# GpSimd in place of ScalarE and SyncE as the asker for half of the gate and value weights

## The chip, the cores and the metric

The kernel runs on one core of a Trainium2 chip. The core's engines are TensorE (PE in the profile; PEld is its weight load), VectorE (DVE), ScalarE (ACT), GpSimd (POOL) and SyncE (SP). Each has its own queue of instructions and works through it in order; semaphores hold an instruction until what it needs is there. SP only asks for transfers here; ScalarE can ask for them too, and so can GpSimd. A transfer that one of them has asked for is carried out by 16 DMA engines, beside all other work. The metric is device time in microseconds (us); the time given for a kernel is the median of its runs.

## What is computed

An mLSTM cell over 4 batches, 8 heads, 768 time steps and a head size of 40, and a gated feed-forward block on its output:

```python
for t in range(S):                     # S = 768, for each batch and head
    m_new = np.maximum(f_gate[:, :, t] + m, i_gate[:, :, t])
    f_stab, i_stab = np.exp(f_gate[:, :, t] + m - m_new), np.exp(i_gate[:, :, t] - m_new)
    C = f_stab[..., None, None] * C + i_stab[..., None, None] * (vt outer kt)
    n = f_stab[..., None] * n + i_stab[..., None] * kt
    y[:, :, t] = sigmoid(o_gate[:, :, t]) * (C @ qt) / np.maximum(np.abs(n @ qt), 1.0)
x = y as (3072, 320)                   # tokens x (heads * head size)
g = x @ w_gate                         # (320, 1536)
out = (g * sigmoid(g) * (x @ w_val)) @ w_out
```

The inputs of the cell are float32. The three weight matrices are float64 in memory, and the kernel makes float32 of them itself.

## The kernel before

The 768 steps are cut into six groups (`NG`) of 128. In each group the cell runs in its parallel form (scores, a weight matrix, a carried state), and the group's 4 x 128 = 512 tokens then go through the feed-forward block. The order of all instructions is written out by hand; nothing is planned by a scheduler, so an engine's queue holds its instructions in the order of the Python calls that touch it.

**The opening, group 0.** Lines 619 to 666 interleave the first group's cell with the arrival of the first weights. Its weight matrix `W0` lies in the tile `h_sb` (blocks 0 to 7), `W0[:, u * H + h]` for batch u and head h; halves P = 0 and 1 are batches 0, 1 and 2, 3. For each half:

- `first_scores` (L565): PE makes scores, and DVE multiplies them into `W0` in place (L575, four instructions).
- `first_values` (L551): GpSimd copies the last column of `W0` (L552) and scales the values by it (L553). It reads that column before L575 of the same half overwrites it.
- `first_own` (L579), once per batch: PE multiplies `W0` with the values (L582). `first_x` (L584) divides on DVE, and `first_gate` (L593) multiplies by the output gate on DVE (L596) and has GpSimd copy 64 columns to the end of each row of `x_sb` (L597).
- `first_seam` (L610): PE transposes `x_sb` (L616), ten transposes of a half in three parts, and ScalarE, ScalarE and DVE copy the parts to `xT`. The last two transposes read the columns that L597 wrote.
- `first_state` (L599): PE, with GpSimd's `vw_sb`, makes the first carried state (L604).

`burn` (L518) is a matmul without use that keeps PE busy.

**The first feed-forward.** `hidden(0, m)` (L698), for the twelve blocks m of 128 hidden features: ten pairs of matmuls (L706), gate on partitions 0 to 63 and value on 64 to 127, then SiLU on ScalarE (L711) and a product on DVE (L712). The dictionaries `slots` and `ahead` say what is put between the blocks.

**Weights.** `PIECES` cuts the gate and value weights into seven pieces, of 1, 1, 2, 2, 2, 2 and 2 blocks, and the output weights into three. `piece_load(p)` (L161) asks for a piece. For a gate/value piece that is three transfers, in this order: the gate half to partitions 0 to 63 (320 rows of 128 or 256 float64), and the value half to partitions 64 to 127 in two parts, four chunks (64 x 4 rows) and one chunk (64 rows). The transfers come from line L187. The raw words go to a buffer named `raw` (two of them in turn, pieces 0, 1, 5 and 6), or to parts of `h_sb` (pieces 2 and 3) and `wo_sb` (piece 4) that are not in use yet. Piece 2's place is under the part of `W0` that batches 1 and 2 and half of batch 0 use, so its requests wait for `first_own(2)`. Pieces 5 and 6 wait until the blocks that lay in their buffer are scaled; all wait for an earlier transfer that had the same completion semaphore. SP and ScalarE draw these in turn from one set of eight, GpSimd from another set of eight.

A block j then becomes float32 in three steps: `scale(j)` (two ScalarE instructions, L212 and L214), `join(j)` (two DVE instructions, L221 and L222) and `rounded(j)` (L229; on GpSimd, and on DVE for blocks 0, 1, 2, 9, 10 and 11).

Pieces 0 to 5 are asked for in the opening (lines 636, 642, 645, 657, 665 and 666), piece 6 in `slots[1]`, after block 1. In the queue of SP the gate halves stand behind the loads of k, q, v and the output gate of group 0, and ahead of the loads of k for group 1, the write of `M_dram`, the loads of q, and (L484) the reading of `M_dram` into `w_sb`.

From group 1 on, the products of the feed-forward use seven multiplications in place of eight (`gated`, L847, and `project_seven`, L755); the change touches nothing there.

Of the kernel before, what the change touches and what calls it, by code (L numbers as in the profile page):

```python
# [24 lines left out]
def kernel(  # L25
# [18 lines left out]
    nc = tc.nc  # L44
# [116 lines left out]
    def piece_load(p, home=None):  # L161
        kind, m, n = PIECES[p]
        if kind == "gv":
            a, d = NKC, n * 128
            gate_w, val_w = (w[:, m * 128:(m + n) * 128].rearrange("(c p) f -> p c f", p=HP) for w in (moe_w_gate, moe_w_val))
            src = [(slice(0, HP), slice(0, NKC), gate_w), (slice(HP, 128), slice(0, NKC - 1), val_w[:, 1:]),
                   (slice(HP, 128), slice(NKC - 1, NKC), val_w[:, 0:1])]
            queues = (nc.sync,) + 2 * (nc.scalar if p < 5 else nc.sync,)
        else:
            a, d = n, DM  # L170
            src = [(slice(0, 128), slice(0, n), moe_w_out[m * 128:(m + n) * 128].rearrange("(a p) d -> p a d", p=128))]
            queues = (nc.sync,)
        if src[0][2].dtype == F32:
            for r, cs, w in src:
                if kind == "o":
                    nc.sync.dma_start(out=wo_sb[r, m:m + n, :], in_=w)
                else:
                    for x in range(n):
                        nc.sync.dma_start(out=wgv_sb[r, m + x, cs], in_=w[:, :, ts(x, 128)])
            return  # L180
        if home is None:
            raw = conv.tile([128, 4 * NKC * 128], U32, name="raw")
        else:
            raw = home.rearrange("p a t -> p (a t)").bitcast(U32)
        raw = raw[:, 0:2 * a * d]
        for (r, cs, w), queue in zip(src, queues):
            queue.dma_start(out=raw[r].rearrange("p (a d) -> p a d", a=a)[:, cs], in_=w.bitcast(U32))  # L187
        words = raw.rearrange("p (a d two) -> p a d two", two=2, a=a)
        raws[p] = (words[:, :, :, 0], words[:, :, :, 1])
        split(p)  # L190
# [4 lines left out]
    def split(p):  # L195
        if p in raws:
            lo, hi = raws.pop(p)
            kind, m, n = PIECES[p]
            if kind == "gv":
                for c in range(n):  # L200
                    r = slice(c * 128, (c + 1) * 128)
                    blocks[m + c] = (lo[:, :, r], hi[:, :, r], wgv_sb[:, m + c])
            else:
                for c in range(0, n, 2):
                    blocks[NFC + (m + c) // 2] = (lo[:, c:c + 2], hi[:, c:c + 2], wo_sb[:, m + c:m + c + 2, :])
# [428 lines left out]
    first_turn(1, q_sb, qT, (A, V))  # L634
    load(o_sb, o_gate, 0, 1)
    piece_load(0)
    first_own(1)
    first_values(1)
    first_scores(1)
    first_x(1)  # L640
    sig(0)
    piece_load(1)
    burn(3)
    first_own(2)
    piece_load(2, h_sb[:, 1:1 + NKC])
    sig(1)
    burn(2)
# [460 lines left out]
```

## Time and profile before

| | us |
|---|---|
| median of three runs | 512.6 |
| the runs | 513.2, 512.21, 512.6 |
| the profiled execution: device time | 513.3 |
| the profiled execution: span, first to last instruction | 511.5 |
| PE busy with L854 for gv_x from xT, 720 matmuls | 89.1 |
| PE busy with L706, 240 matmuls | 53.7 |
| value halves asked for by ScalarE: issue of one, median, into raw, h_sb, wo_sb | 0.65, 0.62, 0.55 |
| the same, from issue to landing, the larger part, into raw, h_sb, wo_sb | 4.0, 9.1, 11.6 |
| value halves asked for by SP: from issue to landing, larger and smaller part | 11.8, 10.4 |
| gate halves, from issue to landing, into raw (320 KB), h_sb, wo_sb, raw (640 KB) | 7.0, 11.7, 15.7, 8.9 |

How to read the profile: times are from the start of the span. A line of the timeline gives the start, the time from there to the end of the merged instructions, the engine, the line of the kernel, the operation, output and inputs, and how many instructions it merges; in brackets stands how long the engine was idle before, and what ended that. SPq and ACTq are the queues of SP and ScalarE, on which a request for a transfer is not counted as busy. A row of the table of windows gives a stretch, its length, then for PE, PEld, DVE, ACT and POOL the busy time and (the number of instructions), then the granted clock of PE, the share of the DMA engines, and GB/s. Ends of matmuls are modelled.

### The profile page before, as it was taken

The page shows a single profiled execution, that of the slowest core. Times are in us where ns is not written, and L with a number is a line of the kernel's source. Part 1 is how long each engine was busy: PE and PEld are TensorE (multiplying, and loading weights), DVE is VectorE, ACT ScalarE, POOL GpSimd, SP SyncE. Part 2 cuts the span into 40 slices and gives each one's busy share as a digit, 9 for nine tenths or more (in the row PEclk, how much of TensorE's full clock was granted, in tenths as well). Part 3 has the DMA queues.
Part 4 walks back from the last instruction along what each step waited for, and adds up shares of the span by engine and source line. Part 5 has one row for each costly group of instructions (what it writes and reads, how often), then busy time and mean ns, then how long its engine had stood idle before and what let it go on. Part 6 is the DMA issues. An engine that isn't in the chain of part 4 may idle for free.

```text
span 511.5 us, 14788 instructions
## 1 busy us (share of the span) xinstructions
PE 505.1 (99%) x6307; PEld 428.8 (84%) x6309; DVE 332.3 (65%) x539; ACT 204.8 (40%) x394; POOL 255.0 (50%) x274
## 2 busy tenths in 40 slices
PE   8999999999999999999999999999999999999997
PEld 4964445667888899988899888899988899988896
DVE  5779767887897777687466678467658554233421
ACT  3477655448512339312339321338421340223210
POOL 1303427475879663367652457652447650166710
PEclk9999999999999999999999999999999999999999
DMA  9999999698502992501993411993101200000001
GB/s 123 174 232 238 168 194 244 148 177 119 88 1 45 143 130 39 92 3 26 156 134 42 75 21 27 156 131 43 42 3 19 37 3 27 27 1 0 1 14 38
DMA packets 205497, 43.27 MB, mean 85 GB/s; under 512 B 193432, under 2 KB 200600, under 8 KB 205432
## 3 DMA queue, kind: packets, MB, share of 16 engines
q1 hardware_dynamic: 203444, 39.49, 49.4%
q10 hardware_dynamic: 1988, 2.85, 2.4%
q8 instruction: 49, 0.80, 0.7%
q14 instruction: 16, 0.13, 0.1%
HBM read 35.68 MB, written 4.01 MB: 78 GB/s over the span
## 4 chain that ended last, share of the span: by engine, by line
PE 91%; DMA 2%; DVE 2%; issue 1%; POOL 1%; ACT 1%; SPq 0%; DVEq 0%; ACTq 0%; POOLq 0%
PE gv_x L854 26%; PE o_ps L777 23%; PE gv_y L854 21%; PE gv_ps L706 5%; PE o_ps L723 5%; DMA w_sb<-M_dram 2%; PE inter L402 2%; PE intra L411 2%; PE sp L353 2%; PE first_y L582 1%; PE add L379 1%; POOL w_sb L493 1%; PE burn L521 1%; PE tp_kq L561 1%; PE sp L571 1%
## 5 line engine op out<-in xcount | busy, mean ns | idle before, releaser
L854 PE MATMUL gv_x<-xT,wgv_sb 64*128 64x256 f32 x720 | 89.1, 377 | 0.0
L854 PEld LDWEIGHTS gv_x<-xT,wgv_sb 64*128 64x128 f32 x720 | 69.6, 187 | 7.9 <-issue 0.2
L777 PE MATMUL o_ps<-wo_sb,h_sb 128*128 128x160 f32 x480 | 67.4, 300 | 0.0
L777 PEld LDWEIGHTS o_ps<-wo_sb,h_sb 128*128 128x128 f32 x480 | 65.6, 190 | 1.7 <-issue 1.7
L902 ACT ACTIVATE h_sb<-gv_x 128x256 f32<-128x256 f32 x30 | 11.5, 383 | 117.8 <-PE gv_x L854 117.8
L706 PE MATMUL gv_ps<-xT,wgv_sb 64*128 64x512 f32 x240 | 53.7, 596 | 0.3 <-DVE wgv_sb L229 0.3
L706 PEld LDWEIGHTS gv_ps<-xT,wgv_sb 64*128 64x128 f32 x240 | 23.6, 187 | 24.4 <-issue 23.2
L854 PE MATMUL gv_y<-q_sb,wgv_sb 64*128 64x256 f32 x360 | 44.0, 377 | 0.0
L854 PE MATMUL gv_y<-xT,wgv_sb 64*128 64x256 f32 x360 | 43.9, 376 | 0.0
L854 PEld LDWEIGHTS gv_y<-q_sb,wgv_sb 64*128 64x128 f32 x360 | 34.9, 187 | 4.2 <-DVE tmp L894 0.4
L854 PEld LDWEIGHTS gv_y<-xT,wgv_sb 64*128 64x128 f32 x360 | 35.0, 187 | 3.9
L364 POOL TENSOR_TENSOR vw_sb<-v_sb,w_sb 128x656 f32<-128x656 f32 x10 | 14.6, 1467 | 41.2 <-ACT w_sb L509 40.0
L777 PE MATMUL o_ps<-wT,S 128*128 128x160 f32 x240 | 33.4, 299 | 0.0
L777 PEld LDWEIGHTS o_ps<-wT,S 128*128 128x128 f32 x240 | 32.9, 190 | 0.0
L509 ACT ACTIVATE w_sb<-w_sb,g_T 128x64 f32<-128x64 f32 x128 | 31.0, 334 | 0.0
L854 PE MATMUL gv_x<-q_sb,sw 64*128 64x256 f32 x240 | 31.0, 376 | 0.0
L875 POOL TENSOR_TENSOR h_sb<-x_sb 128x512 f32<-128x512 f32 x12 | 15.8, 1314 | 24.6 <-ACT x_sb L874 24.6
L895 POOL TENSOR_TENSOR tmp<-tmp 128x512 f32<-128x512 f32 x15 | 20.0, 1332 | 14.5 <-DVE tmp L894 14.5
L875 POOL TENSOR_TENSOR h_sb<-tmp 128x512 f32<-128x512 f32 x13 | 16.5, 1269 | 21.5 <-ACT tmp L874 21.5
L744 POOL TENSOR_TENSOR S<-h_sb 128x256 f32<-128x256 f32 x30 | 22.6, 752 | 9.2 <-DVE h_sb L875 7.3
L854 PE MATMUL gv_y<-q_sb,sw 64*128 64x256 f32 x200 | 27.0, 388 | 0.0
L723 PE MATMUL o_ps<-wo_sb,h_sb 128*128 128x320 f32 x96 | 26.9, 437 | 0.0
(221 smaller groups left out, 984.6 us busy)
## 6 DMA issues: line engine op xcount, KB each, us to landing
w_sb<-M_dram SPq DMA_DIRECT2D x10, 512.0 KB, 7.1
k_sb<-in_k_dram SPq DMA_DIRECT2D x12, 320.0 KB, 7.4
v_sb<-in_v_dram SPq DMA_DIRECT2D x12, 320.0 KB, 5.5
o_sb<-in_o_gate_dram SPq DMA_DIRECT2D x12, 320.0 KB, 6.8
raw<-in_moe_w_out_dram SPq DMA_DIRECT2D x3, 1280.0 KB, 7.5
x_sq<-k_sb SPq DMA_DIRECT2D x64, 40.0 KB, 2.0
q_sb<-in_q_dram SPq DMA_DIRECT2D x32, 64.0 KB, 3.8
out_dram<-tmp SPq DMA_DIRECT2D x24, 80.0 KB, 1.7
```

The costliest lines, as they stand in the source:

```text
L353: nc.tensor.matmul(sp[two][half(i), a, :], lhsT=kT[feats(two), P * UA + a, half(i)], rhs=qT[feats(two), P * UA + a, half(i)], start=True, ...
L364: eng.tensor_tensor(vw_sb[:, heads(P)], v_sb[:, heads(P)], w_sb[:, heads(P), last].to_broadcast([128, UH, D1]), op=ALU.mult)
L402: nc.tensor.matmul(inter[two][half(i), a, :], lhsT=qT[feats(two), P * UA + a, half(i)], rhs=state(2 * n + i)[feats(two), P * UA + a, :], s ...
L509: nc.scalar.activation(w_sb[:, h], w_sb[:, h], AF.Exp, bias=g_T[:, n, h:h + 1], scale=-1.0)
L706: nc.tensor.matmul(ps[i], lhsT=wgv_sb[half(i), m, kc, :], rhs=x[half(i), kc, :], start=(kc == 0), stop=(kc == NKC - 1))
L723: nc.tensor.matmul(ps[u], lhsT=hid(g, m)[:, ts(u, L)], rhs=wo_sb[:, m, :], start=(m == 0), stop=(m == NFC - 1))
L744: eng.tensor_tensor(S1[:, k], lo[:, second_half], hi[:, second_half], op=ALU.add)
L777: nc.tensor.matmul(node[x][:, i], lhsT=lhs(k)[:, ts(i, L)], rhs=rhs(k), start=start and k == 0 and i == 0, stop=stop and k == KH - 1, skip ...
L854: nc.tensor.matmul(ps[:, i, cols], lhsT=lhs(c)[half(i)], rhs=rhs(c)[half(i)], start=start and c == 0, stop=stop and c == n - 1, skip_group ...
L875: (nc.vector if k == KH - 1 else nc.gpsimd).tensor_tensor(h_sb[:, 2 * k + 1], uw[:, 0], uw[:, 1], op=ALU.mult)
L895: nc.gpsimd.tensor_tensor(uw[:, :, second_half], uw[:, :, second_half], uw[:, :, first_half], op=ALU.add)
L902: nc.scalar.activation(h[:, first_half], x[:, 0, first_half], AF.Silu)
```

## The change

In `piece_load`, both parts of the value half of every gate/value piece are asked for by GpSimd. Before, ScalarE asked for those of pieces 0 to 4 and SP for those of pieces 5 and 6. The gate half stays with SP, the output weights too. What is moved, and when `piece_load` is called, stays as it was.

```diff
@@ -165,7 +165,7 @@
             gate_w, val_w = (w[:, m * 128:(m + n) * 128].rearrange("(c p) f -> p c f", p=HP) for w in (moe_w_gate, moe_w_val))
             src = [(slice(0, HP), slice(0, NKC), gate_w), (slice(HP, 128), slice(0, NKC - 1), val_w[:, 1:]),
                    (slice(HP, 128), slice(NKC - 1, NKC), val_w[:, 0:1])]
-            queues = (nc.sync,) + 2 * (nc.scalar if p < 5 else nc.sync,)
+            queues = (nc.sync,) + 2 * (nc.gpsimd,)
         else:
             a, d = n, DM
             src = [(slice(0, 128), slice(0, n), moe_w_out[m * 128:(m + n) * 128].rearrange("(a p) d -> p a d", p=128))]
```

GpSimd's queue holds, from the opening on: L298, the value half of piece 0, L552 and L553 of the second half, piece 1, piece 2, L597 twice, pieces 3, 4 and 5, L229 of block 3, piece 6, L229 of block 4. The orders on PE and DVE stay as they were.

## The prediction

> **What bounds the kernel now.** I read the page's busy shares first, then the table of windows, to see where TensorE (PE) stands still.
>
> ```profile
> span 511.5 us, 14788 instructions
> PE 505.1 (99%) x6307; PEld 428.8 (84%) x6309; DVE 332.3 (65%) x539; ACT 204.8 (40%) x394; POOL 255.0 (50%) x274
> ```
>
> ```profile
> 0.00:12.00 12.00, 10.81 (x62) 5.09 (x63) 6.20 (x22) 3.67 (x7) 2.11 (x11) 1.00 0.96 118
> 12.00:25.00 13.00, 12.58 (x135) 11.53 (x135) 9.78 (x20) 6.02 (x10) 4.84 (x5) 1.00 1.28 173
> 25.00:32.00 7.00, 6.56 (x104) 6.15 (x103) 6.67 (x19) 4.54 (x8) 0.58 (x2) 1.00 1.11 221
> 32.00:50.00 18.00, 18.00 (x90) 8.99 (x90) 14.84 (x26) 13.41 (x19) 3.10 (x2) 1.00 1.06 246
> 80.00:90.00 10.00, 9.74 (x217) 6.05 (x208) 6.11 (x11) 6.39 (x8) 7.30 (x8) 1.00 0.91 179
> 90.00:115.00 25.00, 24.68 (x367) 17.02 (x364) 21.28 (x36) 11.32 (x20) 14.81 (x11) 1.00 1.01 166
> ```
>
> In a window row the first pair is PE's busy time. From 32 us to 400 us PE lacks only 0.26 + 0.32 + 0.10 us, so nearly nothing can be gained there; whatever moves the first L706 matmul moves the end one for one. The granted clock is 1.00 in every window. So I read the opening, 18 to 32 us, in the timeline, first GpSimd's (POOL's) own and then the other engines':
>
> ```profile
> 18.31 1.53 POOL L298 TENSOR_TENSOR i_sb<-i_sb,f_sb 32x640 f32<-32x640 f32 x1
> 19.79 0.19 POOL L552 COPY w_end<-h_sb 128x16 f32<-128x16 f32 x1
> 20.06 1.29 POOL L553 TENSOR_TENSOR vw_sb<-v_sb,w_end 128x656 f32<-128x656 f32 x1
> 25.97 0.29 POOL L597 COPY x_sb<-x_sb 128x128 f32<-128x128 f32 x1 [4.62 <-DVE x_sb L596]
> 29.02 0.29 POOL L597 COPY x_sb<-x_sb 128x128 f32<-128x128 f32 x1 [2.77 <-DVE x_sb L596]
> ```
>
> ```profile
> 21.59 2.48 DVE L575 TENSOR_TENSOR h_sb<-sp,h_sb 128x512 f32<-128x512 f32 x4 [2.18 <-PE sp L571]
> 22.97 1.87 PE L582 MATMUL first_y<-v_sb,h_sb 128*128 128x41 f32 x16
> 25.12 1.88 PE L582 MATMUL first_y<-v_sb,h_sb 128*128 128x41 f32 x16
> 26.82 1.29 PE L616 MATMUL tp_x<-ident,x_sb 128*128 128x128 f32 x10
> 28.08 0.88 DVE L596 TENSOR_TENSOR x_sb<-x_sb,o_sb 128x320 f32<-128x320 f32 x2
> 29.29 0.49 DVE L221 TENSOR_SCALAR wgv_sb<-top 128x640 uint32<-128x640 uint32 x1
> 31.92 17.46 PE L706 MATMUL gv_ps<-xT,wgv_sb 64*128 64x512 f32 x80 [0.28 <-DVE wgv_sb L229]
> ```
>
> The chain of waits follows this path: L575, first_y (twice), then on DVE first_x, L596, the copy of xT, join and rounding of block 0, and L706 at 31.92. POOL has the gaps (21.35 to 25.97, 26.26 to 29.02), and its short copies look harmless. They are not: L552 reads the column of W0 that L575 overwrites, and in both programs as built the first L575 of the second half waits for POOL.
>
> **The change, part by part.** Fourteen DMA requests, two for each of seven gate/value pieces, leave the queues of ScalarE (ten) and SP (four) for POOL.
>
> *Removed from ScalarE and SP.* ScalarE's queue loses 4 x 0.65 + 4 x 0.62 + 2 x 0.55 = 6.2 us, and the sigmoid that sat 4.8 us behind the request for piece 2 runs earlier. That is worth nothing: its result is used by L596 at 28.08, which follows first_x without a gap, and ScalarE's copies of xT wait for the transposes at 26.82. SP loses 4.06 + 1.28 us of issue at 37.04 and 57.96. It also waits less, because the eight completion semaphores that SP and ScalarE take in turn are no longer given to these fourteen: the gate half of piece 5, at 36.40 here after a 6.0 us wait on an earlier transfer, can go out behind piece 4's at about 30.3, and the k, q and M_dram requests follow sooner. The one place that waits for these later is L488, which idled 0.89 us for w_sb<-M_dram before 72.75; behind it, through the mask and the exp, stands the PE wait of 0.2 us at L379 and the loss of 0.26 us in that window. I take -0.3 us (at least 0, at most -0.7, all of PE's lack from 32 to 400).
>
> *Added to POOL: the price.* The trace of before has no DMA request on POOL. From below: a piece costs what it cost on the hardware queues, 2 x 0.62 = 1.24 us. From above: each request is as long as POOL's longest L229, 2.41 us, so 4.8 us a piece. POOL is a software engine here (a 128x640 L229 takes 1.55 us, 2.4 ns an element), so I add to 0.62 us two such steps for each row asked for, one for where it is read and one for where it goes: 256 rows give 0.62 + 1.23 = 1.85, 64 rows 0.62 + 0.31 = 0.93. I take 2.8 us a piece (an estimate, nearer the middle of the ends) and call it g.
>
> The Trainium skill (DMA: Bandwidth & Descriptors, "Latency and other measured facts") gives about 1 us to the first byte for a request by GpSimd and 0.6 us for one by hardware; this trace agrees with the second (0.62 us) and cannot show the first. By the page g would be about 2.0 and the sum 0.3 - 0.3 = 0.0 us, the first rival.
>
> *Where it lies.* In POOL's new order: L298, piece 0, L552, L553, piece 1, piece 2, both L597, pieces 3, 4 and 5, the rounding of block 3, piece 6, the rounding of block 4.
>
> 1. L552 starts at 19.8 + g and ends 0.2 later. L575's second half started at 21.59 and first_y could have been 0.2 us later (two short warming matmuls lie ahead of it on PE). So first_y slips by 20.05 + g - 21.59 - 0.2 = g - 1.7: 1.1 us.
> 2. Piece 1 follows L553 (1.55 us with L552), so it ends at 21.35 + 2g = 26.95. Piece 2 waits for the second-last first_y (24.84 + 1.1, no further delay) and ends at 21.35 + 3g = 29.75. Behind it is L597, which PE needs for the last two L616 transposes. L597 then ends at 21.65 + 3g = 30.05. In before those transposes ran at about 27.9; with them the work behind in PE's order (L604, L616 of the second half, L604) reaches L706 just in time if L597 ends by 28.05. So the slip is 3g - 6.4 = 2.0 us. It contains the 1.1 us, since the later of the two decides.
> 3. Pieces 3 to 5 end at about 31.3 + 3g = 39.7; the next POOL work, the rounding of block 3, came at 43.22. Cover: 3.5 us and the slip; if it were gone, PE's L706 would wait one for one, as it waited 0.58 us for it in before.
> 4. Piece 6 falls between the roundings of blocks 3 and 4: 44.77 + 2.8 = 47.6 against 47.11. Block 4 is then done at 49.1, and its matmuls start at 50.05: no cost, 0.9 us left.
> 5. The values land later by what they are asked for later. Piece 2 is asked for by 29.75, and with the 9.1 us to landing of before is there at 38.9; its first use, ScalarE at 36.98, has slipped to 39.0. Nothing, but with 0.1 us left. Pieces 3 to 6 have 2 us and more.
>
> Sum: 2.0 - 0.3 = **+1.7 us**. Against the profiled execution, 513.3 us with 511.5 of span, that is 515.0. That execution lies 0.7 above the median of the runs, 512.6, so I forecast **514.3 us**. By the ends of g: 1.24 gives no slip and -0.3; 4.8 gives 8.0 - 0.3 = +7.7.
>
> **The rivals.** A difference under 0.2%, 1.0 us, can't be told from none in this kernel.
>
> *POOL asks cheaply: no change, or a little faster.* One mechanism: if g stays under 1.7 us, L552 is back before L575 wants it and all of POOL's requests fit in its gaps, while SP's earlier loads keep their 0.3 us. 512.3 us. With g up to 2.5 the slip is at most 1.1 and the net 0.8: 513.4, still no change. For it: the hardware queue's 0.62 us, and POOL's gaps of 4.6, 2.8 and 13.9 us up to 43.22. Against: it needs 64 strided rows of four parts handled as fast in software as in hardware. Faster by over 0.2% would need more than PE's whole 0.7 us of gaps after 32 us, hence something this profile does not show.
>
> *Late values.* If piece 2 takes 11.7 us to land, as its gate half did in before, ScalarE's scale of block 2 is 2.5 us late. No cover: scale, join and rounding end in L706 of block 2, which already followed the rounding at 40.12 with no gap. 514.3 + 2.5 = 516.8 us. For it: the DMA engines are busy from 12 to 80 us (a share of 1.06 to 1.28 in the windows) and SP's requests come earlier. Against: ScalarE's queue shared the same engines with SP's in before, and its piece 2 took 9.1 us.
>
> *The port.* L221 (0.49 us) took 1.16 and 1.43 us beside POOL instructions in before, at 58.36 and 75.03. After the second L597 (29.02 in before) piece 3 starts on POOL just as L221 of block 0 starts on DVE. If the request goes first and shuts L221 out for its 1.85 us, the chain gets that too: 514.3 + 1.9 = 516.2 us. Against: both follow the same L596, and L221 came 0.02 us earlier than POOL's copy ended.
>
> The Trainium skill (SBUF — State Buffer, "Who interferes with whom") has the two exclude each other for a whole instruction, whoever comes first. The slow L221 rows agree that DVE is held; no run here shows it for a request.
>
> **How the numbers follow.** Forecast (L597 and L552 late, g from 2.5 to 3.7): 0.44. Cheap requests or a slip below 1.0 us: 0.33. Late values: 0.09; the port: 0.07; faster by something unseen: 0.07. So faster 0.07, same 0.33, slower 0.60. The range runs from 511.9 (no slip and all 0.7 us gained) to 519.0 (g of 4.4: 6.8 - 0.3 = 6.5, or a rival on top of the forecast). Of the slower cases alone it is 513.7 to 518.
>
> **What would show it.** POOL's timeline: requests of 1.85 and 0.93 us at 19.8 and after L553 and the first_y; L552 at 22.6 in place of 19.79; L575's second half idle until POOL; L597 at 29.75; L706 at 33.9. Four fewer requests on SP, the gate half of piece 5 near 31, L488 with no wait for DMA. From 34 us on, PE as before. I am wrong if a piece costs POOL under 1.7 us, if L706 starts at 31.9, or if PE gets gaps behind it that it had not.

## The result and the profile after

The kernel after takes 514.77 us (median of 13 runs, 513.6 to 517.03), the kernel before 512.48 us (median of 13 runs of the same comparison, 511.39 to 515.36): a ratio of 1.0039, 95% interval 1.0021 to 1.0057. The forecast was 514.3 us. The number is met; the way to it is another one than the prediction worked out. The medians lie 2.3 us apart and the two profiled executions 1.5 us; what follows explains the 1.5.

The profiled execution after took 514.81 us with a span of 513.0 us, 1.5 us more than before. Its page, in parts 1 and 3 (the queue's packets, MB, and share of 16 engines):

```profile
span 513.0 us, 14804 instructions
...
PE 504.7 (98%) x6307; PEld 429.4 (84%) x6309; DVE 333.0 (65%) x539; ACT 205.0 (40%) x394; POOL 263.4 (51%) x288
...
q1 hardware_dynamic: 202740, 38.18, 47.7%
q0 software_dynamic: 1184, 3.93, 3.3%
```

The queue q0 is new: what GpSimd asks for travels on a queue of its own, in packets of 4 KB. The busy time of the engines is nearly that of before, but for POOL, which now has the fourteen requests (288 instructions, 274 before). PE's loss must therefore be a wait, and the table of windows says where. After:

```profile
25.00:32.00 7.00, 6.66 (x103) 6.14 (x101) 6.66 (x19) 3.68 (x7) 3.69 (x9) 1.00 1.06 217
60.00:80.00 20.00, 18.26 (x134) 10.28 (x132) 14.27 (x17) 11.63 (x18) 6.41 (x4) 1.00 1.14 212
```

and the second stretch before:

```profile
60.00:80.00 20.00, 20.00 (x214) 10.13 (x214) 14.83 (x18) 11.45 (x18) 7.32 (x5) 1.00 1.08 232
```

In 25 to 32 us, where the prediction had put the loss, PE is busy for 6.66 us (6.56 before). In 60 to 80 us it lacks 1.74 us, where before it lacked nothing. The timeline of POOL shows why the opening held:

```profile
19.71 1.33 POOL L187 DMA_DIRECT2D raw<-in_moe_w_val_dram  x2
21.03 0.22 POOL L552 COPY w_end<-h_sb 128x16 f32<-128x16 f32 x1
21.34 1.29 POOL L553 TENSOR_TENSOR vw_sb<-v_sb,w_end 128x656 f32<-128x656 f32 x1
22.57 1.20 POOL L187 DMA_DIRECT2D raw<-in_moe_w_val_dram  x2
...
26.14 0.29 POOL L597 COPY x_sb<-x_sb 128x128 f32<-128x128 f32 x1 [0.28 <-DVE x_sb L596]
...
44.90 1.51 POOL L187 DMA_DIRECT2D raw<-in_moe_w_val_dram  x2
```

A piece (two requests) holds POOL for 1.2 to 1.5 us, not for 2.8. L552 starts 1.2 us later than before and ends at 21.25 us, 0.5 us ahead of the second half of L575 (21.76), and L597 starts 0.2 us later. The wait that did come is one line of the waits of PE:

```profile
PE tp_kq L318 <- DMA q_sb<-in_q_dram: 1.7, 1, 1.7
```

L318 transposes k and q of group 1; q had not landed. The queue of SP shows how q came to be late. Here it is after (start, time of issue):

```profile
30.17 0.60 SPq L187 DMA_DIRECT2D raw<-in_moe_w_gate_dram  x1
31.86 18.81 SPq L138 DMA_DIRECT2D k_sb<-in_k_dram  x2
50.72 6.46 SPq L963 DMA_DIRECT2D M_dram<-M_sb  x1
57.23 2.02 SPq L138 DMA_DIRECT2D q_sb<-in_q_dram  x2
```

and the same requests before:

```profile
41.21 9.97 SPq L138 DMA_DIRECT2D k_sb<-in_k_dram  x2
51.29 2.12 SPq L963 DMA_DIRECT2D M_dram<-M_sb  x1
53.45 2.37 SPq L138 DMA_DIRECT2D q_sb<-in_q_dram  x2
```

k is asked for 9.4 us sooner and is through the queue no sooner: its issue lasts until 50.7 us in place of 51.2. The write of `M_dram` then takes 6.46 us to issue in place of 2.12, so q goes out 3.8 us later. On PE this ends as

```profile
32.10 17.46 PE L706 MATMUL gv_ps<-xT,wgv_sb 64*128 64x512 f32 x80 [0.28 <-DVE wgv_sb L229]
...
61.98 0.71 PE L318 MATMUL tp_kq<-ident,q_sb 64*128 64x64 f32 x16 [1.74 <-DMA q_sb<-in_q_dram]
```

L706 starts 0.18 us later than before, which is no loss worth the name; L318 on q follows its twin on k after a gap of 1.74 us.

What else moved at 50 us? The value half of piece 6. Before, SP asked for it at 57.96 us, behind q. Now POOL asks at 44.90 us, and its 160 packets of 4 KB start between 50.61 and 55.57 us. The rows of k and q have 160 bytes. Counted from the packets in the trace:

| kernel, stretch (us) | packets of 4 KB | rows of 160 B | these rows per us |
|---|---|---|---|
| before, 50.0 to 56.0 | 0 | 4985 | 831 |
| after, 50.61 to 55.57 | 160 | 1204 | 243 |
| after, its middle, 51.5 to 54.0 | 109 | 50 | 20 |

One packet of 4 KB took 0.37 us in the mean and one row 0.028 us, and the 16 DMA engines carry both queues: beside piece 6 the short rows of SP's queue went at under a third of their rate, and in the middle of the stretch they nearly stopped. There the 109 long packets alone make 39.7 of the 40 us that 16 engines have in 2.5 us. What SP asks for next is issued late; e7 below shows that it is this, and no other wait of the write of `M_dram`, that takes the time.

The Trainium skill (DMA: Bandwidth & Descriptors, "Queues, rings and completion order") says that each DMA engine takes turns between the queues it has work for, a packet at a time. The trace agrees in so far as both queues move in the same stretch. Over the whole of it 7.5 rows passed for each long packet, and 3 to 14 in e2, e7 and e10 below; in its middle it was one row for two long packets. Which records make up one turn, the trace does not show.

### The profile page after: what moved, and what is told of

Read it like the earlier page. It is cut to its first block, busy times and chain, and to the rows that moved or that the text cites. A ratio compares the mean times of both kernels' runs of the same rounds, so it can differ in the third digit from the quotient of the medians.

```text
span 513.0 us, 14804 instructions
## 1 busy us (share of the span) xinstructions
PE 504.7 (98%) x6307; PEld 429.4 (84%) x6309; DVE 333.0 (65%) x539; ACT 205.0 (40%) x394; POOL 263.4 (51%) x288
## 3 DMA queue, kind: packets, MB, share of 16 engines
q0 software_dynamic: 1184, 3.93, 3.3%
## 4 chain that ended last, share of the span: by engine, by line
PE 95%; DMA 2%; DVE 2%; ACT 1%; issue 0%; SPq 0%; DVEq 0%
PE gv_x L854 25%; PE o_ps L777 22%; PE gv_y L854 21%; PE gv_ps L706 10%; PE o_ps L723 5%; PE inter L402 2%; PE sp L353 2%; PE intra L411 2%; PE add L379 1%; PE first_y L582 1%; DMA i<-in_i_gate_dram 1%; DMA q_sb<-in_q_dram 1%; PE sp L571 1%; PE tp_kq L561 1%; ACT h_sb L547 0%; PE wps L536 0%
## 5 line engine op out<-in xcount | busy, mean ns | idle before, releaser
L854 PE MATMUL gv_x<-xT,wgv_sb 64*128 64x256 f32 x720 | 89.4, 377 | 0.0
L854 PEld LDWEIGHTS gv_x<-xT,wgv_sb 64*128 64x128 f32 x720 | 69.9, 187 | 7.9 <-issue 0.2
L706 PE MATMUL gv_ps<-xT,wgv_sb 64*128 64x512 f32 x240 | 54.2, 596 | 0.4 <-DVE wgv_sb L229 0.3
L706 PEld LDWEIGHTS gv_ps<-xT,wgv_sb 64*128 64x128 f32 x240 | 24.7, 187 | 23.9 <-issue 22.5
L854 PE MATMUL gv_y<-q_sb,wgv_sb 64*128 64x256 f32 x360 | 44.1, 377 | 0.0
L854 PE MATMUL gv_y<-xT,wgv_sb 64*128 64x256 f32 x360 | 44.0, 376 | 0.0
L854 PEld LDWEIGHTS gv_y<-q_sb,wgv_sb 64*128 64x128 f32 x360 | 35.1, 187 | 4.3 <-DVE tmp L894 0.4
L854 PEld LDWEIGHTS gv_y<-xT,wgv_sb 64*128 64x128 f32 x360 | 35.1, 187 | 3.9
L854 PE MATMUL gv_x<-q_sb,sw 64*128 64x256 f32 x240 | 31.1, 376 | 0.0
L744 POOL TENSOR_TENSOR S<-h_sb 128x256 f32<-128x256 f32 x30 | 22.6, 754 | 9.5 <-DVE h_sb L875 7.6
L854 PE MATMUL gv_y<-q_sb,sw 64*128 64x256 f32 x200 | 27.2, 389 | 0.0
```

The source lines that it names most:

```text
L706: nc.tensor.matmul(ps[i], lhsT=wgv_sb[half(i), m, kc, :], rhs=x[half(i), kc, :], start=(kc == 0), stop=(kc == NKC - 1))
L744: eng.tensor_tensor(S1[:, k], lo[:, second_half], hi[:, second_half], op=ALU.add)
L854: nc.tensor.matmul(ps[:, i, cols], lhsT=lhs(c)[half(i)], rhs=rhs(c)[half(i)], start=start and c == 0, stop=stop and c == n - 1, skip_group ...
```

## The experiments

Three theories were tried. A, the place: piece 6's 640 KB, moved on a second queue beside k, `M_dram` and q, make the loss. B, the opening: the steps 1 and 2 of the prediction (POOL is late with L552 or L597). C, the queue: SP's requests come in another rhythm, whichever piece causes it. In every run the ratio is to the kernel before on the same chip.

To separate where a kernel loses from where it wins time back, I use four landmarks on PE: the starts of the first L706 (end of the opening), of L353 (behind the transposes L318), of L379 (behind `w_sb`), and of the second group of transposes L476. Differences to before, profiled executions; inserted lines shift the numbers in some kernels. At L706 about half a microsecond is scatter: e2, whose opening is that of before, shows +0.44.

| kernel | L706 | L353 | L379 | L476 | span | ratio, 95% |
|---|---|---|---|---|---|---|
| before (us) | 31.92 | 78.75 | 85.27 | 108.75 | 511.5 | |
| after | +0.18 | +2.15 | +2.14 | +1.42 | +1.5 | 1.0039 [1.0021, 1.0057] |
| e1, piece 6 back on SP | +0.31 | +0.31 | +0.30 | -0.17 | +0.2 | 1.0006 [0.9987, 1.0025] |
| e2, only piece 6 | +0.44 | +1.59 | +1.59 | +4.64 | +5.4 | 1.0046 [1.0016, 1.0075] |
| e7, q before `M_dram` | +0.03 | +1.21 | +1.20 | +1.07 | +1.2 | 1.0040 [1.0017, 1.0063] |
| e8, piece 6 earlier | -0.02 | +0.29 | +0.29 | -0.78 | -0.2 | 1.0009 [0.9991, 1.0026] |
| e5, piece 6 later | +0.58 | +0.59 | +0.58 | +0.50 | +1.0 | 1.0024 [0.9999, 1.0049] |
| e10, a fifth of piece 6 | +0.39 | +0.40 | +0.39 | +0.78 | +0.9 | 1.0041 [1.0018, 1.0064] |
| e3, piece 6 by ScalarE | +0.10 | +8.91 | +8.91 | +7.44 | +8.0 | 1.0173 [1.0140, 1.0207] |
| e9, pieces 5 and 6 on SP | -0.06 | -0.04 | +1.04 | +1.24 | +2.5 | 1.0058 [1.0036, 1.0080] |
| e12, `w_sb` before piece 6 | -0.18 | +4.28 | +4.27 | +3.53 | +6.2 | 1.0087 [1.0050, 1.0125] |
| e4, piece 0 in five requests | +4.23 | +4.23 | +4.23 | +2.76 | +3.3 | 1.0042 [1.0019, 1.0066] |
| e11, the same again | +1.42 | +1.43 | +1.43 | +0.14 | +0.2 | 1.0015 [0.9985, 1.0046] |

**e1: the change without piece 6.**

```diff
-            queues = (nc.sync,) + 2 * (nc.gpsimd,)
+            queues = (nc.sync,) + 2 * (nc.sync if p == 6 else nc.gpsimd,)
```

> The changed kernel, with the value half of piece 6 alone asked for by SP again, in its old place behind the loads of q. Theory A (the 640 KB of piece 6, asked for at 44.9 us on a second queue, pass in front of k, M_dram and q, and q comes 1.7 us too late for L318): the wait of L318 for q_sb is gone, q is asked for by 54 us as in before, the ratio to before is 1.000 (0.998 to 1.002). Theory B (the opening: GpSimd's requests hold up L552 and L597): still 1.7 us or more over before. Theory C (SP's queue as a whole is out of step, whichever piece is moved): L318 still waits, by 1 us or more.

513.76 us, and before 513.56. The loss is gone, with six of seven pieces still on POOL. SP's queue and the window:

```profile
50.68 2.08 SPq L963 DMA_DIRECT2D M_dram<-M_sb  x1
52.81 2.81 SPq L138 DMA_DIRECT2D q_sb<-in_q_dram  x2
```

```profile
60.00:80.00 20.00, 20.00 (x203) 10.35 (x203) 15.43 (x18) 11.72 (x18) 7.50 (x5) 1.00 1.11 239
```

`M_dram` takes 2.08 us again and L318 waits for nothing, although k is asked for as early as in the kernel after (31.99 us). B, which needs the pieces of the opening, falls; so does C in the form that any shift of SP's requests costs.

**e2: piece 6 alone.**

```diff
-            queues = (nc.sync,) + 2 * (nc.scalar if p < 5 else nc.sync,)
+            queues = (nc.sync,) + 2 * (nc.gpsimd if p == 6 else nc.scalar if p < 5 else nc.sync,)
```

> The kernel before, with the value half of piece 6 alone asked for by GpSimd, after the rounding of block 3. Theory A: L318 waits for q_sb by 1 to 3 us, q is asked for at 57 us or later, the time is 1.5 to 2.5 us over before (1.003 to 1.005). Theories B and C: no wait for q, 1.000, since the opening and all other requests are those of before.

516.25 against 513.56 us: one piece of seven brings a loss as large as that of the change. The queue of SP and the wait of PE:

```profile
49.02 7.67 SPq L963 DMA_DIRECT2D M_dram<-M_sb  x1
56.75 1.92 SPq L138 DMA_DIRECT2D q_sb<-in_q_dram  x2
```

```profile
61.42 0.72 PE L318 MATMUL tp_kq<-ident,q_sb 64*128 64x64 f32 x16 [0.93 <-DVE h_sb L712]
```

The profile puts the wait down to DVE, but the last landing of q's first load came at 61.29 us, 0.13 ahead of the matmul. L353 is 1.15 us later relative to L706, where it is 1.97 in the kernel after. The rows of k went at 344 per us beside piece 6. The further loss up to L476 (3 us in this execution) is not the same thing: 1.4 of it is a gap at L402 for which the profile shows no releaser, and the granted clock was 0.93 in 90 to 115 us.

**e7: q ahead of `M_dram`.** Is q late only because it stands behind a slow request?

```diff
-            run(nc.sync.dma_start, out=M_dram, in_=flat(M_sb)), run(load_all, q_sb, q, 1)],
+            run(load_all, q_sb, q, 1), run(nc.sync.dma_start, out=M_dram, in_=flat(M_sb))],
```

> The changed kernel with piece 6 on GpSimd at its place, but on SP the two loads of q stand ahead of the write of M_dram. Theory A (piece 6's rows share the engines with k and hold SP's queue up, and M_dram's 6.5 us of issue stood ahead of q): q is asked for near 51 us in place of 57.2 and is there for L318 at 59.6; no wait or under 0.5 us, time 1.000 to 1.002. If what delays q is its own transfer beside piece 6's rows and not its place in SP's queue: L318 still waits, by over 1 us, 1.003 or more.

No: 514.91 against 513.86 us, still 1.0040; the gain that A had promised did not come.

```profile
50.26 7.60 SPq L138 DMA_DIRECT2D q_sb<-in_q_dram  x2
57.97 2.27 SPq L963 DMA_DIRECT2D M_dram<-M_sb  x1
```

Now it is q whose issue takes 7.60 us, and `M_dram`, behind it, has its 2.27 us back. Whichever request meets piece 6 pays. PE waits at L318 for 1.0 us in place of 1.7 (q's first load landed at 60.91 us, 0.14 ahead of it). This run also answers a rival. In the kernel after, the waits of SP's queue put 6.1 us of `M_dram`'s issue down to DVE's L221. Here the first load of q, which waits for no semaphore, stands at the same place and takes 5.09 us, and `M_dram`'s wait for L221 is 1.6 us. So the time was not DVE's.

**e8: piece 6 asked for right behind piece 5**, at about 34 us (its gate half stays in its place):

```diff
@@ piece_load (the loop becomes a function `ask` over `parts`; cut here)
...
+        if p == 6:
+            ask(parts[1:])
+            raws["p6"] = lambda: ask(parts[:1])
+        else:
+            ask(parts)
@@ opening
     piece_load(5)
+    piece_load(6)
@@ slots
-        1: [run(piece_load, 6), run(late_decay)],
+        1: [lambda: raws.pop("p6")(), run(late_decay)],
```

> The changed kernel, with the value half of piece 6 asked for by GpSimd right after piece 5 (near 34 us in place of 44.9); its gate half stays in its place on SP. The same 640 KB still go ahead of k. If it is being beside k's, M_dram's and q's short rows that costs (the two together moved 155 KB a us from 50 to 56 us, long rows alone 275): the rows now go beside the long rows of the gate halves, k starts about 2.3 us later than in before, near 49.5, SP asks for q by 55.5, and L318 waits by under 0.7 us; 1.000 to 1.002. If it is the order alone (any 640 KB ahead of k): L318 waits by 1.5 us or more, as in the changed kernel, 1.003 or more.

513.75 against 513.86 us. All seven pieces are asked for by GpSimd, as in the change, and nothing is lost:

```profile
52.47 2.31 SPq L972 DMA_DIRECT2D M_dram<-M_sb  x1
54.83 2.44 SPq L138 DMA_DIRECT2D q_sb<-in_q_dram  x2
```

Its 640 KB travel directly behind piece 5's, and the second queue is empty by 52.04 us, before `M_dram` goes out. This run is the clearest for A.

**e5: piece 6 asked for later**, behind `cap_table` at 56 us:

```diff
@@ piece_load (`ask` and `parts` as in e8; cut here)
...
+        if p == 6:
+            ask(parts[:1])
+            live["p6"] = lambda: ask(parts[1:])
+        else:
+            ask(parts)
@@ slots
-        4: [run(decay), run(cap_table)],
+        4: [run(decay), run(cap_table), lambda: live.pop("p6")()],
```

> The changed kernel, all values still asked for by GpSimd, but that of piece 6 after cap_table (near 56 us in place of 44.9); its gate half stays where it is. Theory A: q is asked for by 54 us, L318 doesn't wait, 1.000 to 1.002; the value half lands 9 to 13 us later, at 66 to 69 us, so ScalarE's scale of block 10, at 68.1 in before, may wait a little, with no more than 0.5 us on PE. Theory B: 1.7 us or more over before. If GpSimd as the asker costs by itself, whenever it asks: 1.003 or more.

515.0 us. `M_dram` takes 2.06 us, q goes out at 52.52, L318 waits for nothing, and from L706 to L379 the kernel keeps its distance to before (+0.58, +0.59, +0.58). That is as A has it; the ratio, 1.0024 with an interval from 0.9999, does not decide alone.

**e10: only the smaller of piece 6's two requests (128 KB) by GpSimd.**

```diff
-            queues = (nc.sync,) + 2 * (nc.gpsimd,)
+            queues = (nc.sync, nc.sync if p == 6 else nc.gpsimd, nc.gpsimd)
```

> The kernel after, with piece 6's larger value request (512 KB of its 640) back on SP; GpSimd asks only for the smaller one (128 KB). Theory A (long rows of a second queue beside k's, M_dram's and q's short ones; cost grows with their bytes): M_dram's issue 2.1 to 3.5 us in place of 6.46, q asked by 54.5, L318 waits under 0.5 us, ratio 1.000 to 1.002, span 511.5 to 512.2. If the presence of any request on the second queue at 45 us costs, whatever its size: M_dram's issue above 5 us, q asked after 56, L318 waits 1 to 1.7 us, ratio 1.003 to 1.005, span near 513.

In the trace it went as A said: `M_dram` 2.62 us, q at 53.32, no wait at L318, the four landmarks +0.39, +0.40, +0.39, +0.78. The ratio, 1.0041, did not: it is as high as that of the change. Of the 0.9 us of the profiled execution, 0.4 are there before L706 and 0.4 come behind L379, in gaps of 0.37 and 0.61 us on PE that the profile puts down to no releaser. Such gaps of 0.2 to 1.4 us, between 86 and 101 us, are in before too (0.32). The runs fall into two clumps, spans of 512.2 to 513.0 and of 514.0 to 516.9; what the second have, no trace here shows (of the 29 runs of before beside them, five have a span above 513.5). So the size of the effect against bytes stays open.

**e3: piece 6 by ScalarE**, to tell a second queue of any kind from GpSimd's:

```diff
-            queues = (nc.sync,) + 2 * (nc.gpsimd,)
+            queues = (nc.sync,) + 2 * (nc.scalar if p == 6 else nc.gpsimd,)
```

> The changed kernel, with the value half of piece 6 asked for by ScalarE, a hardware queue, at the same place in the program (after block 1, near 41 to 45 us). Theory A in its broad form (any second queue lets these rows pass in front): L318 waits for q_sb by 1 to 2.5 us, as in the changed kernel, 1.003 to 1.005. Theory A in its narrow form (it needs GpSimd's queue, whose packets carry 4 KB where the hardware queues' carry 2 KB): the wait is half of that or less, under 1 us.

522.55 us, by a wait that I had not foreseen and that hides the answer. The timeline of ScalarE and the waits of PE:

```profile
41.85 10.85 ACTq L187 DMA_DIRECT2D raw<-in_moe_w_val_dram  x2
52.87 0.78 ACT L212 ACTIVATE top<-h_sb 128x640 f32<-128x640 f32 x1 [11.40 <-DMA raw<-in_moe_w_gate_dram]
```

```profile
PE tp_g L677 <- ACT keep L963: 7.0, 1, 7.0
```

The second request stood on ScalarE's queue, waiting for an earlier transfer with the same completion semaphore, and ScalarE computed nothing for 11.4 us (the gate half of piece 5 landed at 52.16 us, and the request went out at 52.19). `M_dram` issued in 1.90 us and q went out at 53.43: most of piece 6's packets ran ahead of k's rows (47.11 to 50.78 us), so the times say nothing on the two forms of A. The packets say a little. ScalarE's second request did meet short rows: in 54.5 to 55.5 us 142 rows of 160 bytes went beside 54 packets of 2 KB, where 1793 had gone in the 2 us ahead. `M_dram`'s own longer rows stand there too, but in the kernel before, with them alone, no microsecond at that place has under 292. That points to the broad form; one microsecond of one trace does not show it. On POOL no request stood like that for an earlier transfer in any run.

**e6 and e9: pieces 5 and 6 back on SP.** By A this had to be as good as e1.

```diff
-            queues = (nc.sync,) + 2 * (nc.gpsimd,)
+            queues = (nc.sync,) + 2 * (nc.gpsimd if p < 5 else nc.sync,)
```

> GpSimd asks for the values of pieces 0 to 4, SP for those of 5 and 6 as before: only the requests that ScalarE made are moved. Theory A: no wait at L318, all as in e1, 0.999 to 1.001. It could be a little faster than before, by the 0.2 us wait at L379 and the stretches near it, but PE has no more than 0.7 us of gaps to give, so not by over 0.2%. The opening's theory with the prediction's price: 1.003.

515.27 against 513.86 us, 1.0034 [1.0019, 1.0049]: a miss. e9 is the same kernel once more, with a trace at the full clock.

> The kernel of e6 (pieces 0 to 4 by GpSimd, 5 and 6 on SP) once more, since that run left no trace that can be compared and a ratio of 1.0034 that no theory had asked for. If only piece 6 beside k and q costs (theory A): ratio 0.999 to 1.0015, span 511.3 to 512.3, no wait of L318 for q_sb, PE busy 19.9 or more of 20 us in 60 to 80. If piece 5's two requests on SP cost by themselves (rival): ratio 1.002 to 1.005, span 513 to 515; then L318, or L379/L488, shows a wait of 1 to 2 us, or PE loses as much before 45 us, because k is asked at 34.6 in place of 31.9 us. If the first run's ratio was scatter: as under A.

516.69 against 513.59 us, 1.0058. This is the rival of that expectation, but at another place than it named:

```profile
52.38 2.33 SPq L963 DMA_DIRECT2D M_dram<-M_sb  x1
54.76 2.20 SPq L138 DMA_DIRECT2D q_sb<-in_q_dram  x2
...
60.49 8.60 SPq L484 DMA_DIRECT2D w_sb<-M_dram  x2
```

```profile
73.88 2.36 DVE L488 TENSOR_TENSOR w_sb<-g_T,w_sb 128x1024 f32<-128x1024 f32 x2 [0.49 <-DMA w_sb<-M_dram]
```

```profile
86.31 0.31 PE L379 MATMUL add<-vw_sb,k_sb 64*64 64x41 f32 x2 [0.17 <-DVE w_sb L360]
86.91 2.33 PE L379 MATMUL add<-vw_sb,k_sb 64*64 64x41 f32 x126 [0.29 <-DVE w_sb L360]
```

The same places before:

```profile
59.33 8.22 SPq L484 DMA_DIRECT2D w_sb<-M_dram  x2
72.75 2.36 DVE L488 TENSOR_TENSOR w_sb<-g_T,w_sb 128x1024 f32<-128x1024 f32 x2 [0.89 <-DMA w_sb<-M_dram]
85.78 2.33 PE L379 MATMUL add<-vw_sb,k_sb 64*64 64x41 f32 x126 [0.20 <-DVE w_sb L360]
```

q is in time: L353 starts 0.04 us earlier than before. But with piece 5 and 6 ahead of it on SP, L484 asks for `w_sb` at 60.49 us, 1.16 later than before; L488 starts 1.13 us later; and through the mask on POOL, the exp on ScalarE and L360, L379's larger part starts at 86.91 in place of 85.78. `w_sb` is not alone in this. SP also asks for piece 6's values 1.15 us later (59.11), ScalarE waits 2.73 us for them (1.14 before), and DVE, behind it, is ready for L488 only at 73.39 in place of 71.86. Had `w_sb` been in time, L488 would still have started 0.6 us late. So C is right after all in a narrower form: not each shift on SP's queue costs, but one of 1.2 us that reaches `w_sb` and piece 6 does, since DVE and ScalarE already waited 0.89 and 1.14 us for them before. Another 1.2 us is lost behind L476 (0.47 of it at L854, on L395); its source is not shown.

**e12: `w_sb` ahead of piece 6**, to test that:

```diff
-        1: [run(piece_load, 6), run(late_decay)],
-        2: [..., run(decay_rows), run(weights_load, 1), run(load_all, v_sb, v, 1)],
+        1: [run(weights_load, 1), run(piece_load, 6), run(late_decay)],
+        2: [..., run(decay_rows), run(load_all, v_sb, v, 1)],
```

> The kernel of e9 with weights_load(1) (L484) asked on SP ahead of piece 6's three requests. In e9 the trace put its loss at L488: w_sb asked at 60.49 us (59.33 before), landed 1.2 us later, and POOL's mask, ACT's L512, DVE's L712 and L360 and PE's L379 each started 1.1 us later. If that is the cause: w_sb asked at 56.5 to 57.5, L488 has no wait for DMA and starts by 72.7, L379's second matmul at 85.5 to 86.0, ratio 0.999 to 1.003, span 511.3 to 512.8. If w_sb's place was only a sign of other contention (k's longer issue, 19.78 us, itself): L379 still 1 us late, ratio 1.004 or more, span near 514. A new loss is possible if piece 6, now asked after w_sb, lands after its rounding at 74 us: then DVE or ACT waits for raw.

518.8 against 514.71 us. `w_sb` is asked for at 56.94 us and L488 no longer waits for it, but the loss that was named as possible came and hides the rest. ScalarE waits for piece 6:

```profile
73.06 0.78 ACT L212 ACTIVATE top<-raw 128x640 f32<-128x640 f32 x1 [6.25 <-DMA raw<-in_moe_w_val_dram]
```

Piece 6's value half, now asked for at 64.05 us (57.96 before), lands 6.25 us after ScalarE wanted it. So the cause of e9 rests on its trace; e12 moved the wait from `w_sb` to piece 6 and did not confirm it.

**e4 and e11: piece 0 made dear.** Was the opening safe because a piece is cheap, or because the prediction's chain does not exist? Piece 6 back on SP, and piece 0's larger part cut into four requests:

```diff
+            queues = (nc.sync,) + 2 * (nc.sync if p == 6 else nc.gpsimd,)
+            if p == 0:
+                src[1:2] = [(slice(HP, 128), slice(c, c + 1), val_w[:, c + 1:c + 2]) for c in range(NKC - 1)]
+                queues = (nc.sync,) + 5 * (nc.gpsimd,)
```

> As e1 (piece 6 back on SP), but the larger value part of piece 0 is asked for in four requests of one chunk, so GpSimd has five requests ahead of L552 in place of two. At 0.55 to 0.65 us each (the changed kernel's profile has 0.54 to 0.67) they take 3.0 us in place of 1.33, so g for piece 0 passes the 1.7 us at which the prediction's first slip begins. The opening's theory, with only its price wrong: L552 at 22.7, the second half of L575 starts after it and near 23.0 in place of 21.7, first_y and L706 slip by 1.0 to 1.3 us (L706 at 33.1 to 33.5), the time is 1.0 to 1.3 us over e1's, 1.002 to 1.003 of before. If the opening has other slack that the prediction didn't see: L706 stays at 32.0 to 32.4.

> The kernel of e4 (e1 with piece 0's larger value part cut into four requests) once more: there PE stood 1.0 us at L575's second half, and TensorE's granted clock was 0.54 in 25 to 32 us. If the gap on PE at 22 to 23 us brings the lower clock: again under 0.8 in 25 to 32, span 514 to 515, ratio 1.003 to 1.006. If the lower clock was chance: 1.0 in 25 to 32, and the span is 511.7 and the gap, 512.5 to 513, ratio 1.001 to 1.003. In both, the copy at L555 starts at 22.0 to 22.6 and DVE waits for it.

e4 gave 516.37 against 513.86 us, e11 513.95 against 513.59. In both, five requests took POOL 2.7 us, nearly the price that the prediction had put on a piece. The timelines of POOL, DVE and PE in e11:

```profile
20.02 2.73 POOL L190 DMA_DIRECT2D raw<-in_moe_w_val_dram  x5
22.74 0.22 POOL L555 COPY w_end<-h_sb 128x16 f32<-128x16 f32 x1
```

```profile
22.99 2.48 DVE L578 TENSOR_TENSOR h_sb<-sp,h_sb 128x512 f32<-128x512 f32 x4 [3.37 <-POOL w_end L555]
```

```profile
23.74 0.81 PE L524 MATMUL burn<-junk 128*128 128x512 bf16 x3 [1.15 <-DVE h_sb L578]
```

The chain is there: DVE waits for POOL's copy, PE stands for 1.15 us (1.04 in e4), and step 1 of the prediction gives 2.74 - 1.7 = 1.0. But the end did not follow. In e11 L706 starts 1.42 us later than before, and so do L353 and L379; at L476 0.14 us are left, and 0.2 at the end. The 1.3 us are won back at two places where PE waits in the kernel before: L379's 128 matmuls take 2.77 us there and 2.01 in e11, and the second 64 of L411 1.61 and 1.05. In e4 the granted clock fell as well:

```profile
25.00:32.00 7.00, 7.00 (x36) 6.44 (x35) 4.55 (x17) 0.77 (x2) 1.49 (x4) 0.54 1.05 210
```

0.54 in 25 to 32 us, which with the gap made 4.2 us at L706. In e11's profiled execution it stayed at 1.00 there. Over both runs, 6 of 24 executions had a mean clock of 0.993 or less, and none of the 63 executions of the kernel before beside them. That speaks for a link between the gap on PE at 23 us and the clock. Other traces here have such places too: e2, with a gap of 1.40 us at 98 us, has 0.81 in 97 to 106; e3, with its 7.0 us, 0.75 in 49 to 58, and all of its six executions have a mean of 0.993 or less; e12, with gaps of 0.71 and 0.66 us, 0.84 in 70 to 80. But the 1.74 us of the kernel after and the 1.15 us of e11 went by at 1.00. So a lower clock came with some gaps and not with others, and what decides is not shown.

## Why the prediction was right in its number and wrong in its cause

- **The price g is the step that failed.** "I take 2.8 us a piece": measured 1.33, 1.20, 1.17, 1.22, 1.16, 1.16 and 1.51 us. The lower bound, two requests as on the hardware queues (1.24), was the right row. The two steps of 2.4 ns for each row asked for have no counterpart: the request for 256 rows took 0.63 us and that for 64 rows 0.54 (piece 2), and five of 64 rows each 0.55. The 0.62 us that the prediction set beside a first-byte time is how long a request holds its queue, and not that time: in the kernel before, the first packet came 1.49 and 0.73 us after ScalarE's requests at 18.29 and 31.94 us, when its queue was empty.
- **Steps 1 and 2 (2.0 us) did not occur.** With g = 1.33 the prediction's own formulas, g - 1.7 and 3g - 6.4, give no slip, and there is none: L552 at 21.03 (said: 22.6), L597 at 26.14 (said: 29.75), L706 at 32.10 (said: 33.9). The threshold itself is real; e4 and e11 pass it, with 2.74 and 2.73 us and gaps of 1.04 and 1.15 us.
- **"Whatever moves the first L706 matmul moves the end one for one"** was too strong. e11 moved it by 1.42 us and the span by 0.2. Some 1.3 us of it were won back at L379 and L411, where before has waits of its own that do not move along. So even the slip of the forecast would probably have brought less than its 2.0 us.
- **"The k, q and M_dram requests follow sooner" failed**, and with it the -0.3 us. The gate half of piece 5 did go out at 30.17 and k at 31.86, as said. But k's issue lasted until 50.7 us, and q went out 3.8 us later than before, not sooner. L488's wait for `w_sb` is gone as forecast, but L488 starts 0.9 us later than before (73.7), and nothing was won. In e1 and e8, without the meeting, 0.5 and 1.1 us are won between L379 and L476; their spans still lie within 0.2 us of before.
- **Step 4, "piece 6 ... no cost", hides the real term.** It weighed piece 6 on POOL's time (44.90 to 46.41 us, and it did cost nothing there) and not on the DMA engines, where it moved from behind q to beside k. That term is 1.74 us at L318, +1.97 from L706 to L353, of which 0.7 are won back by L476.
- **Steps 3 and 5 held**: the rounding of block 3 and the uses of pieces 0 to 5 came as before.
- **The rivals.** Cheap requests was right in its condition, g under 1.7 us, and wrong in its time, 512.3, which rested on the gain at L379. Late values did not come for piece 2. The port did not show: L221 of block 0 took 0.50 us beside piece 3's requests on POOL (0.49 before).

So 514.3 was met by luck: a slip of 2.0 us that did not occur stood in for a wait of 1.74 us that was not in the sum. e1 and e8 show the forecast of the right reasoning: without piece 6's meeting, no change.

No version here beats the kernel before; e8, which keeps the whole change and asks for one piece earlier, equals it as far as its interval can tell.

## What to carry to other kernels

When a transfer changes its asker, its place among the other transfers changes too, and that can cost more than the request does: list what the DMA engines carry at the new time and ask who waits for it. Here the long packets of a second queue (GpSimd's) slowed the short rows of the first, and the requests queued behind those short rows paid, not the transfer that was moved. Before pricing an unknown operation, test the forecast at both ends of its price: here the low end left no slip at all, and the search should then have gone on to the transfers.

## What the runs showed of the hardware

- A request on GpSimd's queue held POOL for 0.54 to 0.82 us (median 0.65 for those into `raw`), about as on ScalarE (medians 0.55 to 0.65), with little dependence on its rows; piece 6's two took 1.51.
- GpSimd's transfers moved rows of 1 and 2 KB in packets of 4 KB on a queue of their own (q0: 960 of its 1184 packets, 3.93 MB; the others hold a few bytes), where ScalarE's queue had packets of the rows' size (q10 before: 640 of 1 KB and 960 of 2 KB).
- A transfer's start can lag: piece 6's first packet came 5.7 us after the request in the kernel after and 4.1 us in e2, but piece 0's and e5's piece 6's 1.7 us after theirs. It is not GpSimd's alone: in e3, on ScalarE's empty queue, it came after 5.3 us. What the longer lag waits for, the traces don't show; it is what put piece 6 just beside k.
- Rows of 160 B alone moved at 130 KB per us (before, 50 to 56 us), and beside 4 KB packets both together at 167 (after, 50.61 to 55.57); rows of 2 KB and more alone at 281 (after, 44 to 47 us). Short rows are the dear ones here, and in 44 to 73 us k, `M_dram`, q, `w_sb` and piece 6 have little slack between them: several orders that delayed one of them by 1 us or more came out on PE, as q in after, e2 and e7, as `w_sb` and piece 6 in e9, as piece 6 in e12.
